# Batch 2 of a sliding-window attention plus mixer kernel: unpadded scores in two bursts, its u transposed by DMA

## The chip, the core and the metric

The kernel runs on one core of a Trainium2 chip. A core has five instruction streams that run beside each other and wait for each other by semaphores: TensorE (PE, matrix products out of SBUF into PSUM; a weight load goes ahead of each matmul), VectorE (DVE), ScalarE (ACT), GpSimd (POOL) and SyncE (SP, which here only issues DMAs). PSUM has eight banks of 2 KB in each partition. The metric is device time in microseconds (us), as the median of several runs; a run with the profiler on gives the trace, and has its own time.

## The reference

q, k and v are 8 batches x 8 heads x 576 positions x 64. Heads 0 to 3 see the last 32 positions; heads 4 to 7 see every fourth of the last 128. The attention output, 576 x 512 a batch, is the x of one mixer block: a token mix, then a channel mix.

```python
scores = scale * np.matmul(q, k.transpose(0, 1, 3, 2))
rel = pos[:, None] - pos[None, :]
mask_plain = (rel >= 0) & (rel < window)                       # window 32, heads 0-3
mask_dil = (rel >= 0) & (rel < window * dilation) & (rel % dilation == 0)   # dilation 4, heads 4-7
attn = softmax(where(mask, scores, -1e9)); x = attn @ v
h = np.maximum(xt @ w_tok1, 0.0) @ w_tok2                      # xt: x transposed, over 576 positions
u = x + h.transpose(0, 2, 1)
h2 = np.maximum(u @ w_ch1, 0.0) @ w_ch2                        # 512 -> 1536 -> 512
return u + h2
```

## The kernel before

All operands of matmuls are fp16, sums are fp32 in PSUM. A batch passes through these steps, each with its tile names:

- **Loads** (SP): q and k as `l_q`, `l_k` (two halves each), `lt` (last 64 positions of both), v as `l_vn`, `l_vt`, `l_vd`, `l_vx`. POOL casts them to fp16 (`c_q`, `c_k`, `c_t`, `vv`, `vt`).
- **Turning** q and k so that the 64 channels lie in the partitions, two heads (a pair `hp`) on top of each other. Batches 0 to 2 use PE transposes into PSUM (`tp_q`, `tp_k`), and DVE or ACT copy them out: keys to `kt`, queries to `qz`, which holds each head of the pair padded with zeros in the other head's 64 rows. From batch 3 on (`by_dma`) DMA transposes issued by SP write `qt`, `kr` and `tt`, and POOL places `kt` from them.
- **Scores**. Batches 0 to 2 (`scores_plain`, `scores_dil`) multiply over 128 rows, one head at a time, the padding hiding the other head; a piece is three yields for a pair: head 0, head 1, and a small bank `sm`. From batch 3 on `scores_twin` (line 465) multiplies over 64 rows: the two heads of a pair are two matmuls on the two halves of the array, one right behind the other. It does two pairs at a stretch (a burst) into six banks; two bursts make a batch. ACT exponentiates out of PSUM into `attp`, `attd`, `attt`, and POOL multiplies by the masks.
- **Values** (`values`): probabilities times v, with a row sum as the 65th column, into `av`; DVE takes the reciprocal (`rec`) and scales to `xn`. Heads 0 to 3 fill the first 256 columns of `xn`, heads 4 to 7 the others.
- **Token mix**: `h1p` (`emit_h1`, one call for 128 hidden units and 256 columns; so all eight heads are in before the last two calls), a relu to `h1`, then `up` (`emit_u`, blocks 4, 0, 1, 2, 3 of the positions), and u = `up` + `xn` as `u16` (blocks 0 to 3) and `u16t` (block 4, for two batches).
- **u transposed** (`uT`): batches 0 to 2 by PE (`emit_uT`, bank `tpu`), from batch 3 on (`turned`) by DMA transposes into `utm` and `utt`, of which ACT copies two quarters into `utd`.
- **Channel mix** (`gen_main`): twelve `gp` groups of four matmuls of 512 columns, each with a relu to `gt`; then `yp`, groups of twelve matmuls of 256 columns, DVE adds u into `o`, and SP stores it. An odd batch also does the block 4 of itself and of the batch before (`gt` tails, three groups of 16, and `yp` of block 4).

The order of the work is written out: for each batch b, `interleave` runs `gen_main(b)` (the channel mix, whose yields count modelled PE microseconds) and puts in between them the steps of later batches, each at a time t of that count: turning and scores of batch b+2, values, token mix and uT of batch b+1, casts and loads of batches b+2 and b+3. Each engine runs its own instructions in the order in which they were written, and SP is one such list too.

Banks: tag `fl` has three, `main` three, `sc` two, each handed round in turn. A tile in a bank waits until what was in it three tiles (`sc`: two) earlier has been read out. `h1p`, `up`, `av`, `tp` and `tpu` are in `fl`; `gp`, `gt` tails and `yp` are in `main`; a burst takes `sc`, `sc`, `fl`, `fl`, `fl`, `main`.

## Time and profile before

| | before |
|---|---|
| median of 3 runs | 290.61 us (290.55 to 290.86) |
| the profiled execution: its time, its span | 291.14 us, 289.2 us |
| mean granted TensorE clock | 0.997 |
| PE busy | 279.6 us, 97% of the span |
| ACT, DVE, POOL busy | 137.1, 130.0, 165.6 us |
| DMA | 52.11 MB, mean 180 GB/s |

In the timeline view each row is a group of like instructions: the start of the first (us from the span's start), the time from there to the end of the last, engine, line, operation, output and input tiles with sizes, the count, and in brackets the idle time before it and what ended it. Matmuls overlap: the next begins while the one before still drains. So the step from one row's start to the next row's start, and not the duration, says how long PE was held.

### The profile page before, as it was taken

How to read it: one execution, taken by the hardware profiler on the slowest of the kernel's cores; microseconds unless marked ns; L12 is line 12 of the kernel's file. 1: busy time of each engine (PE TensorE's matmuls, PEld its weight loads, DVE VectorE, ACT ScalarE, POOL GpSimd, SP SyncE). 2: the span in 40 equal slices, each digit the busy share in tenths (PEclk: the TensorE clock that was granted, in tenths of full speed). 3: DMA queues.
4: the chain of work that ended last, by engine and by line, in shares of the span. 5: the costliest groups of instructions: out<-in, count | busy, mean ns of one | idle time of the engine just before them, and what ended most of it. 6: DMA issues, size and time to landing. Idle time of an engine off the chain costs nothing.

```text
span 289.2 us, 7086 instructions
## 1 busy us (share of the span) xinstructions
PE 279.6 (97%) x2854; PEld 213.5 (74%) x2854; DVE 130.0 (45%) x275; ACT 137.1 (47%) x270; POOL 165.6 (57%) x227
## 2 busy tenths in 40 slices
PE   6999999999999999999999999999999999999994
PEld 2786576897676886688776976697776966896594
DVE  6775659356624138413741155415540274421022
ACT  2874572257553703574447614482446524225500
POOL 6980860576996599649962999279953920000000
PEclk9999999999999999999999999999999999999998
DMA  7999999973998987569897999399965220431023
GB/s 217 267 220 261 252 209 215 319 199 103 312 218 182 325 226 184 74 131 354 206 204 147 331 270 151 62 220 331 216 123 99 80 73 2 90 112 37 2 74 108
DMA packets 103472, 52.11 MB, mean 180 GB/s; under 512 B 71792, under 2 KB 102384, under 8 KB 103440
## 3 DMA queue, kind: packets, MB, share of 16 engines
q1 hardware_dynamic: 99200, 46.55, 64.8%
q0 software_dynamic: 2640, 3.94, 8.0%
q10 hardware_dynamic: 1600, 1.18, 1.4%
q8 instruction: 22, 0.36, 0.5%
q14 instruction: 10, 0.08, 0.1%
HBM read 37.07 MB, written 9.44 MB: 161 GB/s over the span
## 4 chain that ended last, share of the span: by engine, by line
PE 65%; DVE 1%; issue 0%
PE yp L735 25%; PE gp L716 22%; PE up L590 3%; PE gt L707 3%; PE yp L755 3%; PE h1p L578 3%; PE sc L475 2%; PE av L554 1%; PE h1p L576 1%; PE av L559 1%; PE up L601 1%; PE av L552 1%; PE yq L735 0%; PE av L564 0%; PE av L562 0%; DVE xn L112 0%
## 5 line engine op out<-in xcount | busy, mean ns | idle before, releaser
L735 PE MATMUL yp<-w,gt 128*128 128x256 f16 x756 | 87.4, 273 | 0.0
L106 ACT ACTIVATE gt<-gp 128x512 f16<-128x512 f32 x76 | 45.4, 597 | 79.9 <-PE gp L716 79.5
L735 PEld LDWEIGHTS <-gt 128*128 128x128 f16 x768 | 78.6, 106 | 6.3
L716 PEld LDWEIGHTS <-w 128*128 128x128 f16 x384 | 39.0, 114 | 19.6 <-issue 0.5
L112 POOL TENSOR_TENSOR attp<-attp,const 128x1280 f16<-128x1280 f16 x12 | 31.4, 2614 | 34.1 <-ACT attp L499 30.0
L745 DVE TENSOR_TENSOR o<-yp,u 128x512 f32<-128x512 f32 x31 | 21.5, 692 | 64.2 <-PE yp L735 57.0
L716 PE MATMUL gp<-utd,w 128*128 128x512 f16 x120 | 45.5, 380 | 0.0
L716 PE MATMUL gp<-utm,w 128*128 128x512 f16 x120 | 45.5, 379 | 0.0
L716 PE MATMUL gp<-uT,w 128*128 128x512 f16 x144 | 38.7, 379 | 0.0
L112 DVE TENSOR_TENSOR xn<-av,rec 128x320 f16<-128x320 f32 x64 | 31.5, 492 | 2.2
L112 POOL TENSOR_TENSOR attd<-attd,const 128x1024 f16<-128x1024 f16 x12 | 25.3, 2126 | 0.0
L596 DVE TENSOR_TENSOR u<-up,xn 128x512 f16<-128x512 f32 x26 | 17.9, 691 | 8.4 <-PE up L590 8.4
L102 POOL CAST c_q<-l_q 128x512 f16<-128x512 f32 x31 | 19.1, 619 | 2.8 <-DMA l_q<-in_q_dram 2.1
L102 POOL CAST c_k<-l_k 128x512 f16<-128x512 f32 x29 | 17.8, 616 | 1.9 <-DMA l_k<-in_k_dram 1.8
L567 DVE RECIPROCAL rec<-av 128x5 f32<-128x5 f32 x64 | 12.2, 191 | 14.9 <-PE av L564 14.7
L108 DVE TENSOR_SCALAR gt<-gp 128x512 f16<-128x512 f32 x20 | 13.7, 686 | 10.5 <-PE gp L716 10.1
L106 ACT ACTIVATE h<-h1p 128x256 f16<-128x256 f32 x29 | 11.1, 384 | 13.4 <-PE h1p L578 12.9
L392 PEld LDWEIGHTS <-kt 128*128 128x128 f16 x144 | 12.1, 103 | 3.9 <-DVE kt L314 1.4
L499 ACT ACTIVATE attp<-sc 128x480 f16<-128x480 f32 (+1 forms) x30 | 13.4, 526 | 3.0 <-PE sc L475 3.0
L366 POOL COPY kt<-kr 128x512 f16<-128x512 f16 x10 | 10.7, 1075 | 6.2 <-DMA kr<-c_k 6.1
L112 POOL TENSOR_TENSOR attt<-attt,const 128x512 f16<-128x512 f16 (+1 forms) x14 | 14.2, 1016 | 0.0
L605 DVE TENSOR_TENSOR u16t<-up,xn 64x512 f16<-64x512 f32 x7 | 4.8, 689 | 19.6 <-PE up L601 19.6
(135 smaller groups left out, 479.9 us busy)
## 6 DMA issues: line engine op xcount, KB each, us to landing
out_dram<-o SPq DMA_DIRECT2D x72, 128.0 KB, 2.7
l_q<-in_q_dram SPq DMA_DIRECT2D x15, 512.0 KB, 7.2
l_k<-in_k_dram SPq DMA_DIRECT2D x14, 512.0 KB, 7.5
l_vn<-in_v_dram SPq DMA_DIRECT2D x32, 128.0 KB, 6.3
l_vd<-in_v_dram SPq DMA_DIRECT2D x16, 256.0 KB, 4.5
w<-in_moe_w_ch_dram POOLq DMA_DIRECT2D x6, 512.0 KB, 7.6
lt<-in_q_dram SPq DMA_DIRECT2D x8, 128.0 KB, 4.3
l_vt<-in_v_dram SPq DMA_DIRECT2D x8, 128.0 KB, 4.7
```

The costliest lines, as they stand in the source:

```text
L102: eng.tensor_copy(out=out, in_=in_)
L106: nc.scalar.activation(out=out, in_=in_, func=AF.Relu)
L108: eng.tensor_scalar_max(out=out, in0=in_, scalar1=0.0)
L112: eng.tensor_tensor(out=out, in0=x, in1=y, op=ALU.mult)
L366: nc.gpsimd.tensor_copy(out=natural(kt[hp][:, 0:512]), in_=kra[:, hp].rearrange("p r m -> p m r"))
L392: nc.tensor.matmul(out=out, lhsT=lhsT, rhs=qz[hp][:, h, queries], start=hide is None, stop=True)
L499: nc.scalar.activation(out=out, in_=in_, func=AF.Exp, scale=0.125)
L567: nc.vector.reciprocal(out=rec[:, :, 0], in_=av[:, :, 64])
L596: nc.vector.tensor_tensor(out=u16(b, s), in0=blocks4(p), in1=blocks4(xn[b][:, s]), op=ALU.add)
L716: nc.tensor.matmul(out=p, lhsT=w3_block(cb, mb), rhs=uT[(b, cb)][0], start=(i == 0), stop=(i == 3))
L735: nc.tensor.matmul(out=p[:, c], lhsT=gta[:, mb, a0:m0 + 512:4] if half else gta[:, mb, a0:a0 + 128], rhs=w4[mb][:, c], start=(mb == 0), st ...
L745: nc.vector.tensor_tensor(out=blocks4(o32), in0=blocks4(p), in1=u16(b, s), op=ALU.add)
```

## The change

Batch 2 leaves the padded form. Its q and k are still turned by PE (`bare_steps`), but copied unpadded into `qt`, `kr`, `tt` and `kt`, and its scores are two bursts of `scores_twin`. The first burst (pairs 0 and 1) lies in `gen_main(0)`, between the blocks of batch 1's u and its transposes; the second (pairs 2 and 3) lies near the start of `gen_main(1)`. For batch 2 a burst takes `fl` for its first two banks and `sc` for the next two. `scores_twin` now yields after each exponential, and ACT begins with the bank of the tag `main` in every batch from 2 on. Batch 2's u goes by DMA transpose (`turned` is `b >= 2`); its steps, and with them everything else of stage 1, get new times. In stage 1 DVE takes nine of the twelve relus of `gp` (two before), and ACT takes four casts of batch 3's q from POOL. In batch 1 the quarter `cb == 3` of uT is copied by DVE and no longer by ACT.

```diff
+    def twinned(b):
+        return b >= 2
...
+    def bare_steps(b):
+
+        def tails():
+            p = bank("fl", 3, f"tp_t_{b}", FP16)
+            for hp in range(4):
+                nc.tensor.transpose(
+                    out=p[:, 128 * hp:128 * hp + 128],
+                    in_=c16[(b, "t")][:, 2 * hp:2 * hp + 2, :].rearrange("m h d -> m (h d)"), identity=ident)
+            t = p[:, 0:512].rearrange("p (x c) -> p x c", c=128)
+            nc.vector.tensor_copy(out=kta[:, :, 512:S], in_=t[:, :, 64:128])
+            nc.scalar.copy(out=tta, in_=t)
+
+        def turn_over(nm, hp):
+            p = bank("fl", 3, f"tp_{nm}_{b}_{hp}", FP16)
+            for r in range(4):
+                nc.tensor.transpose(
+                    out=p[:, 128 * r:128 * r + 128],
+                    in_=c16[(b, nm)][:, hp, r].rearrange("m h d -> m (h d)"), identity=ident)
+            grid = p[:, 0:512].rearrange("p (r m) -> p r m", r=4)
+            if nm == "q":
+                nc.scalar.copy(out=qta[:, hp], in_=grid)
+            elif hp < 2:
+                nc.vector.tensor_copy(out=natural(kt[hp][:, 0:512]), in_=grid.rearrange("p r m -> p m r"))
+            else:
+                nc.vector.tensor_copy(out=kra[:, hp], in_=grid)
+                nc.vector.tensor_copy(out=natural(kt[hp][:, 384:512]),
+                                      in_=grid[:, :, 96:128].rearrange("p r m -> p m r"))
...
     def scores_twin(b, g):
         tags = (("sc", 2), ("sc", 2), ("fl", 3), ("fl", 3), ("fl", 3), ("main", 3))
+        if b == 2:
+            tags = tags[2:4] + tags[0:2] + tags[4:6]
...
+        yield from small_exps(1)
+        if b == 2:
+            yield from small_exps(0)
+        for hp in (2 * g, 2 * g + 1):
+            for h in range(2):
+                main(hp, h)
+                if h and (g or b == 2):
+                    mask(hp)
+                    if b == 2 and hp % 2 == 0:
+                        mask_tails()
+                yield 0.0
+        if b > 2:
+            yield from small_exps(0)
...
     def emit_uT(b, cb):
-        eng = nc.scalar if cb == 2 or (b and cb == 3) else nc.vector
+        eng = nc.scalar if cb == 2 else nc.vector
...
     def turned(b):
-        return b >= 3
+        return b >= 2
...
     def gen_main(b):
-            relu(nc.vector if (mb % 2 == 1 if b == 0 else mb in (1, 5)) else nc.scalar, gta[:, mb, m0:m0 + 512], p)
+            relu(nc.vector if (mb % 2 == 1 if b == 0 else mb % 4 != 3 if b == 1 else mb in (1, 5)) else nc.scalar, gta[:, mb, m0:m0 + 512], p)
...
         if b == 0:
+            steps += mix_steps(1, 18.0, 20.6, 22.6, 31.4, 1.1)
+            steps += at(24.0, 0.3, cast_steps(2))
+            bare = bare_steps(2)
+            scores2 = score_steps(2, 29.6, 4.4, lag=0.25)
+            steps += [(t, 0.25, f) for t, f in zip((25.2, 25.9, 27.0, 27.6, 28.2, 34.8, 35.2, 35.6, 36.0), bare)]
+            steps += scores2[:10]
+            steps += at(34.0, 0.0, [lambda: emit_loads_qk(3)])
         elif b == 1:
+            va = value_steps(2, 0.0, 1.0)
+            steps += [(0.8 + 0.4 * i, c, f) for i, (_, c, f) in enumerate(scores2[10:])]
+            steps += [(t, c, f) for t, (_, c, f) in zip((2.2, 3.0, 4.8, 5.6, 8.2, 9.0, 10.4, 11.2), va)]
+            steps += mix_steps(2, 7.0, 12.4, 14.6, 24.4, 1.0, 5.6, 0.8)
+            steps += [(9.5 + 1.0 * i, 0.0, lambda i=i: cast_qk(3, "q", i, nc.scalar)) for i in range(4)]
+            steps += score_steps(3, 21.0, 4.6, lag=0.1)
+            steps += at(6.0, 0.0, [lambda: load_v(3)]) + at(20.8, 0.9, load_steps(4))
+            steps += at(11.0, 0.9, dma_steps(3)) + at(17.0, 0.4, place_steps(3))
```

Three places of the order follow. In tile names the first number after the name is the batch; `sc_2_0_5` is bank 5 of batch 2's burst 0, `up_1_2` is block 2 of batch 1's u, `tpu_1_2` its quarter 2 transposed. The last number is only the buffer's.

ACT, at the end of `gen_main(0)`, before:

```order
L594 CAST u16_1_1065<-up_1_2_1097 128x4x128
L100 COPY uT_1_2_1129<-tpu_1_2_1128 128x640
L100 COPY uT_1_3_1165<-tpu_1_3_1164 128x640
L100 COPY qz_64<-tp_q_2_0_1189 64x576 x2
L100 COPY kt_65<-tp_q_2_0_1189 128x64
L100 COPY qz_64<-tp_q_2_1_1221 64x576 x2
L100 COPY kt_65<-tp_q_2_1_1221 128x64
L428 ACTIVATE attp_73<-sc_2_0_0_1238 128x3x160
```

and with the change:

```order
L643 CAST u16_1_1065<-up_1_2_1113 128x4x128
L383 COPY qt_66<-tp_q_2_1_1139 128x512
L534 ACTIVATE attp_73<-sc_2_0_5_1172 128x2x128
L534 ACTIVATE attt_76<-sc_2_0_5_1172 128x2x2x64
L534 ACTIVATE attp_73<-sc_2_0_4_1171 128x2x128
L534 ACTIVATE attt_76<-sc_2_0_4_1171 128x2x2x64
L534 ACTIVATE attp_73<-sc_2_0_0_1167 128x3x160
L534 ACTIVATE attp_73<-sc_2_0_1_1168 128x3x160
L534 ACTIVATE attp_73<-sc_2_0_2_1169 128x3x160
L100 COPY uT_1_2_1224<-tpu_1_2_1223 128x640
L534 ACTIVATE attp_73<-sc_2_0_3_1170 128x3x160
```

Seven exponentials now stand ahead of the copy of batch 1's first transposed quarter. `tpu_1_2` takes the bank that `sc_2_0_0` had.

DVE, in `gen_main(1)`, up to the scaling of batch 2's last head, before:

```order
L112 TENSOR_TENSOR xn_2_1377<-av_2_4_1508,rec_2_4_1515 128x5x64
L108 TENSOR_SCALAR gt_93<-gp_1_5_1505 128x512
L567 RECIPROCAL rec_2_5_1532<-av_2_5_1525 128x5
L112 TENSOR_TENSOR xn_2_1377<-av_2_5_1525,rec_2_5_1532 128x5x64
L567 RECIPROCAL rec_2_6_1565<-av_2_6_1558 128x5
L112 TENSOR_TENSOR xn_2_1377<-av_2_6_1558,rec_2_6_1565 128x5x64
L567 RECIPROCAL rec_2_7_1594<-av_2_7_1587 128x5
L112 TENSOR_TENSOR xn_2_1377<-av_2_7_1587,rec_2_7_1594 128x5x64
```

and with the change:

```order
L112 TENSOR_TENSOR xn_2_1391<-av_2_4_1520,rec_2_4_1527 128x5x64
L108 TENSOR_SCALAR gt_93<-gp_1_5_1509 128x512
L616 RECIPROCAL rec_2_5_1540<-av_2_5_1533 128x5
L112 TENSOR_TENSOR xn_2_1391<-av_2_5_1533,rec_2_5_1540 128x5x64
L108 TENSOR_SCALAR gt_93<-gp_1_6_1546 128x512
L616 RECIPROCAL rec_2_6_1578<-av_2_6_1571 128x5
L112 TENSOR_TENSOR xn_2_1391<-av_2_6_1571,rec_2_6_1578 128x5x64
L616 RECIPROCAL rec_2_7_1591<-av_2_7_1584 128x5
L112 TENSOR_TENSOR xn_2_1391<-av_2_7_1584,rec_2_7_1591 128x5x64
```

The relu of `gp_1_6` now stands among the last heads, and those of `gp_1_0`, `gp_1_2` and `gp_1_4` stand ahead of this piece.

SP, from the loads of batch 3 to those of batch 4, with the change:

```order
L190 DMA l_k_3_1_1273<-in_k_dram 128x4x256
L803 DMA out_0_dram<-o32_0_3_1296 128x256 x2
L207 DMA l_vn_3_1482<-in_v_dram 128x4x64 x4
L207 DMA l_vt_3_1485<-in_v_dram 64x8x64
L207 DMA l_vd_3_1483<-in_v_dram 128x2x256 x2
L207 DMA l_vx_3_1484<-in_v_dram 128x4x64
L351 DMA_TRANSPOSE tt_68<-c_t_3_1480 128x4x128
L351 DMA_TRANSPOSE qt_66<-c_q_3_1544 128x8x128
L351 DMA_TRANSPOSE kr_67<-c_k_3_1507 128x8x128
L351 DMA_TRANSPOSE qt_66<-c_q_3_1544 128x8x128
L351 DMA_TRANSPOSE kr_67<-c_k_3_1507 128x8x128
L687 DMA_TRANSPOSE utm0_89<-u16_2_1648 128x16x128
```

Two things moved here. The store of batch 0's last block (`o32_0_3`) stood ahead of batch 3's q and k and now stands behind them; and the transpose of batch 2's u is new, ahead of batch 4's first load, which follows this piece.

More of the change, by code (lines that the diff above doesn't have):

```diff
@@ L358, in dma_steps @@
         return steps
+    def bare_steps(b):
[23 more added lines that the diff above has]
+                                      in_=grid[:, :, 96:128].rearrange("p r m -> p m r"))
+        return [tails] + [lambda nm=nm, hp=hp: turn_over(nm, hp) for hp in range(4) for nm in ("q", "k")]
     def place_steps(b):
@@ L648, in uT_place, with score_steps @@
             nc.scalar.copy(out=natural(uTd[:, cb - 2]), in_=uTm[i][:, cb].rearrange("p r m -> p m r"))
-    def score_steps(b, t0, dt, offs=(0.0, 0.7, 2.0), places=None):
+    def score_steps(b, t0, dt, offs=(0.0, 0.7, 2.0), places=None, lag=0.0):
         steps = []
-        if by_dma(b):
+        if twinned(b):
             for g in range(2):
-                for i, f in enumerate([scores_twin(b, g)] * 2):
-                    steps.append((t0 + g * dt, 0.86 * (i == 0), lambda f=f: next(f)))
+                f = scores_twin(b, g)
+                at = t0 + g * dt
+                steps.append((at, 0.86, lambda f=f: next(f)))
+                for i in range(7 if g else 9):
+                    steps.append((at + lag * (i + 1), 0.0, lambda f=f: next(f)))
             return steps
@@ L675, in value_steps, with mix_steps @@
         return steps
[L677 removed]
+    def mix_steps(b, t_h1, t_h1b, t_u, t_uT, du=1.0, turn=6.0, gap=2.6):
         h1 = [sb.tile([128, DM], FP16, tag="h1", bufs=4, name=f"h1_{b}_{jb}") for jb in range(2)]
```

80 lines of the change are left out of this document (34 added, 46 removed).

## The prediction

> **What bounds the kernel now.** First the page's part 1, then the busy time by stage: the stretch that the change rewrites (from batch 1's second block of u, at 54.65 us, to batch 2's first `gp`, at 106.39 us) and the rest after it.
>
> ```profile
> PE 279.6 (97%) x2854; PEld 213.5 (74%) x2854; DVE 130.0 (45%) x275; ACT 137.1 (47%) x270; POOL 165.6 (57%) x227
> 55.00:107.00 52.00, 51.19 (x563) 41.29 (x561) 23.25 (x48) 27.33 (x56) 40.53 (x50) 1.00 0.88 224
> 107.00:285.00 178.00, 177.82 (x1721) 134.99 (x1718) 70.07 (x145) 81.40 (x155) 94.68 (x114) 1.00 0.62 150
> ```
>
> PE is busy in 177.82 of the last 178.00 us, at a granted clock of 1.00, and no other engine reaches two thirds. So the end moves with PE alone: what is taken off PE's list before 106.39 us, or added to its waits, comes out at the end one for one, as long as the later stages find their inputs in time. Busy hides waits under about 0.2 us, since a matmul's duration overlaps the next; I take the steps between starts in PE's timeline instead.
>
> ```profile
> 54.65 0.38 PE L590 MATMUL up<-h,w 128*128 128x256 f16 x2
> ...
> 68.30 0.37 PE L392 MATMUL sc<-qz,kt 128*128 128x160 f16 x3
> 68.50 0.39 PE L309 MATMUL tp_k<-const,c_k 128*128 128x128 f16 x4
> ...
> 69.16 0.39 PE L392 MATMUL sm<-qz,kt 128*128 128x128 f16 x6
> 69.39 0.60 PE L716 MATMUL gp<-uT,w 128*128 128x512 f16 x2
> ...
> 70.96 0.39 PE L392 MATMUL sc<-qz,kt 128*128 128x128 f16 x4
> 71.19 0.39 PE L309 MATMUL tp_k<-const,c_k 128*128 128x128 f16 x4
> ...
> 71.68 0.28 PE L392 MATMUL sm<-qz,kt 128*128 128x64 f16 x4
> 71.80 0.60 PE L716 MATMUL gp<-uT,w 128*128 128x512 f16 x2
> ...
> 89.89 0.33 PE L624 MATMUL tpu<-const,u 128*128 128x128 f16 x3
> 90.41 0.23 PE L624 MATMUL tpu<-const,u 128*128 128x128 f16 x1 [0.19 <-DVE u L596]
> ...
> 91.34 0.39 PE L615 MATMUL tpu<-const,u 128*128 128x128 f16 x4
> 91.56 1.03 PE L755 MATMUL yp<-w,gt 128*128 128x512 f16 x4
> 92.42 0.39 PE L624 MATMUL tpu<-const,u 128*128 128x128 f16 x4
> ...
> 93.83 0.59 PE L475 MATMUL sc<-qt,kt 64*128 64x160 f16 x12
> 94.79 0.23 PE L475 MATMUL sc<-qt,kt 64*128 64x128 f16 x2 [0.37 <-DVE uT L102]
> ...
> 98.52 8.03 PE L735 MATMUL yp<-w,gt 128*128 128x256 f16 x72
> 106.39 0.59 PE L716 MATMUL gp<-uT,w 128*128 128x512 f16 x2
> ...
> 123.71 0.64 PE L475 MATMUL sc<-qt,kt 64*128 64x160 f16 x14
> ...
> 124.46 3.45 PE L735 MATMUL yp<-w,gt 128*128 128x256 f16 x30
> 127.84 0.62 PE L475 MATMUL sc<-qt,kr 64*128 64x128 f16 x16
> ...
> 128.51 1.72 PE L735 MATMUL yp<-w,gt 128*128 128x256 f16 x14
> ```
>
> PE's pace without waits is 0.109 us for 256 columns (72 from 98.52 to 106.39), 0.216 for 512 (4 from 91.56 to 92.42), 0.056 for 128 (4 from 91.34 to 91.56). The stretch lasts 106.39 - 54.65 = 51.74 us.
>
> **Work taken off PE.** *Scores.* A padded score piece holds PE 0.20 us (three of 160 columns), 0.23 (the small bank of a plain pair), 0.23 (four of 128) or 0.12 (its small bank). Batch 2 has 4, 2, 4 and 2 of them: 0.80 + 0.46 + 0.92 + 0.24 = 2.42 us. The bursts that replace them are the code of batch 4's, seen above: the second starts 0.10 us after the 30 `yp` matmuls ahead of it are through (124.46 + 30 x 0.109 = 127.74) and the next `yp` starts at 128.51, so it holds PE 0.77 us; the first 124.46 - 123.71 + 0.10 = 0.85. Together 1.62, a gain of **0.80 us**. The Trainium skill, in TensorEngine Tiling (Array Packing), Theoretical Speedup, gives two row tiles up to twice the speed; an estimate from that page would be 1.21 us, and a gain of 0.40 more. The rows contain the 0.1 us on either side of a burst, and I go by them.
>
> *Turning q and k.* 36 transposes before, 36 after: nothing. *u of batch 2.* Its 16 transposes (four groups of 0.22 us by the row at 91.34) leave PE: **0.90 us**. All else on PE's list in the stretch is the same by count. The work goes down by 1.70 us.
>
> **Waits that go.** The same counts give the old work of the stretch: 218 matmuls of 256 columns 23.8 us, 62 of 512 13.4, 120 of 128 (scores left out) 6.7, 60 of 65 at 0.03 1.8, scores 2.42, batch 3's bursts 1.62, in all 49.8. So PE waited 51.74 - 49.8 = **1.95 us** there. The two largest show above: 90.41, where three transposes should have held PE 0.17 us and took 0.52 (the last block of u was not added yet, 0.35), and 94.79 (twelve matmuls of a burst at some 0.034 should be through at 94.24; the banks of uT were still being copied, 0.55). All of these belong to code that is gone or has moved.
>
> **Waits that come.** I walk PE's new list from 54.65 with these rows of ACT, DVE, SP and POOL.
>
> ```profile
> 94.31 2.23 ACT L499 ACTIVATE attp<-sc 128x480 f16<-128x480 f32 x5 [0.87 <-PE sc L475]
> 96.39 0.43 ACT L499 ACTIVATE attt<-sc 128x256 f16<-128x256 f32 x1
> 96.65 0.44 ACT L499 ACTIVATE attp<-sc 128x256 f16<-128x256 f32 x1
> ...
> 98.34 2.06 ACT L499 ACTIVATE attd<-sc 128x512 f16<-128x512 f32 x4 [0.97 <-PE sc L475]
> ...
> 81.24 0.20 PE L564 MATMUL av<-vv,attt 128*128 128x65 f16 x1
> ...
> 81.48 0.20 DVE L567 RECIPROCAL rec<-av 128x5 f32<-128x5 f32 x1 [0.36 <-PE av L564]
> 81.71 0.49 DVE L112 TENSOR_TENSOR xn<-av,rec 128x320 f16<-128x320 f32 x1
> ...
> 70.14 0.68 DVE L108 TENSOR_SCALAR gt<-gp 128x512 f16<-128x512 f32 x1
> 70.74 0.91 DVE L102 COPY qz<-tp_q 64x576 f16<-64x576 f16 x2
> ...
> 68.54 0.61 SPq L196 DMA_DIRECT2D lt<-in_q_dram  x1
> ...
> 83.02 1.32 SPq L348 DMA_TRANSPOSE tt<-c_t  x1
> ...
> 63.21 0.41 POOL L102 CAST vt<-l_vx 128x256 f16<-128x256 f32 x1
> 67.67 2.61 POOL L112 TENSOR_TENSOR attp<-attp,const 128x1280 f16<-128x1280 f16 x1 [4.05 <-ACT attp L437]
> ...
> 89.19 1.07 POOL L366 COPY kt<-kr 128x512 f16<-128x512 f16 x1 [1.19 <-DMA kr<-c_k]
> ...
> 90.55 1.07 POOL L366 COPY kt<-kr 128x512 f16<-128x512 f16 x1
> ```
>
> A large exponential takes a step of 0.52 us in a row and 0.60 alone, a small one 0.27; a reader starts 0.24 us after the start of the last short matmul it waits for (81.24, 81.48); a relu on DVE takes a step of 0.60, a head (`rec` and `xn`) 0.63.
>
> (a) PE's new list up to the first burst is 4.6 us of work, so the burst would begin at 59.3. The six banks that it and the six groups just ahead of it need come back every 0.6 us or so; one, of `up_1_2` on ACT, is late by my walk: **0.2 us**. The burst runs 59.5 to 60.2.
>
> (b) Twelve `yp` matmuls later, at 61.6, `tpu_1_2` wants the bank of `sc_2_0_0`. ACT can start on the burst at 60.4, does four small exponentials (to 61.5) and then that one: free at 62.1, **0.5 us**. The queue behind it on PE is the whole of u's transposes; the next banks come back in time for them.
>
> (c) The second burst ends at 70.35, `gp_1_1` at 71.2, and `av_2_0` wants the bank of `sc_2_1_0`: ACT starts at 70.5, two small ones, then it: 71.65. **0.45 us**. The masks are not the limit: POOL's last cast of batch 2 ended at 63.62, where the burst's exponentials are nearly done, and a mask takes it 2.61 us; with the tails' mask behind it the first pair is ready some 4 us before it is needed.
>
> (d) The last two calls of `h1p` want all eight heads scaled. PE gets there at 81.5. DVE has `gp_1_5`'s relu from 78.7, then head 5, the relu of `gp_1_6`, heads 6 and 7: 0.60 + 0.63 + 0.60 + 0.63 + 0.69 with a short gap ahead of head 6 makes 81.95. **0.45 us**; behind it wait u of batch 2 and its transpose by DMA, which by my walk is copied out some 7 us before the first `gp` of batch 2.
>
> (e) Batch 3's first burst now stands before eight of the twelve matmuls of block 4's `yp`: PE reaches it at 90.5, where it was 93.83, and wants the second `kt` 0.2 us later. That copy ended at 91.62 (90.55 + 1.07). SP sends batch 3's q and k ahead of `o32_0_3` now, by my walk at 66.7 (68.54 before), but that store, about 1 us of issue, then stands ahead of v; so the transposes that began at 83.02 begin some 0.85 us earlier and `kt` is there at 90.8. **0.1 us**; bounds 0 and 0.9 (nothing gained on SP).
>
> With 0.4 us for small waits that such a walk does not see (as the two rows account for 0.90 of the old 1.95, small ones are common here), the new waits come to 0.2 + 0.5 + 0.45 + 0.45 + 0.1 + 0.4 = **2.1 us**; bounds 0 and twice that, since a wait of half a microsecond is worked out from steps that each err by 0.1 or 0.2.
>
> *At nothing:* seven more relus on DVE in stage 1 (its tasks from 69.6 to 82 sum to some 9 of 12.4 us, the relus 0.60 each; their cost where they come late is d); four casts of 0.6 us on ACT, in gaps of the relus that it gave up; the transpose of u ahead of batch 4's loads, which holds SP some 2 us: those loads are cast only after POOL's masks, which end after 104 us, and would have to come 6 us late to be seen.
>
> **Sum.** -1.70 of work, -1.95 of old waits, +2.1 of new ones: **-1.55 us**. The profiled execution took 291.14 us with a span of 289.2, and its 0.5 us over the median of 290.61 and what lies outside the span should not change: 290.61 - 1.55 = **289.05 us**.
>
> **The rivals.**
> 1. *The new waits do not come.* If the banks and DVE keep up, only small waits of 0.5 us remain: -1.70 - 1.95 + 0.5 = -3.15, 287.5 us. For it: after 107 us PE lost 0.2 us in 178. Against: (b) and (c) follow from the order of exponentials and their steps.
> 2. *Emptying PSUM becomes the bound.* All banks of a burst come back only when the whole burst has been read: 4 x 0.27 + 4 x 0.52 = 3.2 us for the first, 2.6 for the second, so `tpu_1_2` would wait 2.0 and `av_2_0` 1.9, that is 2.95 more: 292.0 us, slower. It decides from a wait of some 3.6 us in all. Against it: each tile's bank is handed on by itself. The Trainium skill, on the same page under PSUM Bottleneck, says that array tiles speed up TensorE but not the emptying of PSUM, which may become the limit, and wants ScalarE and VectorE both on it; here ACT alone reads the bursts.
> 3. *Batch 3's keys come late.* Four casts of its q now wait in ACT's list between relus, and SP holds `qt` and, behind it, `kr` until they are done. At 0.85 us early I have the first `kr` land at 88.3; each microsecond later is a microsecond of PE at the burst. It decides from 90.0 on (then the kernel is no faster); at 91.2, as if the second cast were done at 85 and not at 82, the time is 289.05 + 2.75 = 291.8 us, slower. Against: ACT has some 2 us of room there.
> 4. *DVE runs late in stage 1, or the pairs of batch 2 do not overlap as batch 4's do.* DVE's six relus ahead of the last head are 3.6 us, two of them were there before; if its gaps take up half of the 2.4 that are new, (d) is 1.2 and not 0.45; with 0.4 of the same kind at the adds of u, 290.2 us: no change to be seen.
>
> **How the numbers follow.** Forecast 0.55 (its own range, with new waits between 1.2 and 3.0 us, 288.1 to 290.0), rival 1 0.18, rival 2 0.05, rival 3 0.08, rival 4 0.14. A change of 0.2%, 0.58 us, is about what a measurement of this kernel can tell from none. Faster than 290.03: forecast and rival 1, 0.73; slower than 291.19: rivals 2 and 3, 0.13; the rest 0.14. The range takes rival 1's time and rival 4's with some room: 287.4 to 290.8.
>
> **What would show it.** In the changed profile PE's busy time falls by some 1.5 us and its bursts of batch 2 step through in 0.65 to 0.75 us. PE's rows show waits on ACT `attp` before the first `tpu` and on ACT `attd` before the first `av` of batch 2, on DVE `xn` before the third `h1p`, and the first burst of batch 3 begins near 90.5 with little wait on POOL. Batch 2's first `gp` comes near 104.8. I am wrong if those waits sum to under 1 or over 3.5 us, if that burst waits on POOL or DMA for more than 1 us, or if waits turn up after 107 us.

## The result, and the profile after

The changed kernel takes 288.74 us, the median of 4 runs (288.18 to 289.66), against 290.58 us for the kernel before (290.13 to 290.86): a ratio of 0.994, 95% interval 0.9915 to 0.9966. Measured again in the first round of experiments it took 288.2 us (6 runs, 287.65 to 289.31) against 290.35, ratio 0.9921 (0.9899 to 0.9942). It is faster by some 2 us; the forecast was 289.05, so 1.55.

Its profiled execution took 289.66 us with a span of 287.8. The busy time from the page's part 1, then the windows view of the rewritten stretch and of the rest:

```profile
PE 276.8 (96%) x2838; PEld 210.9 (73%) x2838; DVE 132.1 (46%) x278; ACT 134.0 (47%) x265; POOL 163.0 (57%) x221
```

```profile
55.00:105.00 50.00, 49.29 (x544) 38.94 (x542) 25.20 (x50) 24.64 (x52) 38.77 (x44) 1.00 0.92 228
106.00:284.00 178.00, 177.82 (x1715) 135.09 (x1713) 69.73 (x144) 81.41 (x155) 93.51 (x113) 1.00 0.65 154
```

The second row is the old one again: 177.82 busy of 178.00. From batch 2's first `gp` to the last matmul's start it is 178.90 us in both kernels, so nothing of what was won before that point was lost after it. What happened lies in the stretch, in PE's timeline of the changed kernel:

```profile
55.18 0.38 PE L639 MATMUL up<-h,w 128*128 128x256 f16 x2
...
58.10 0.38 PE L378 MATMUL tp_k<-const,c_k 128*128 128x128 f16 x4
58.59 0.38 PE L378 MATMUL tp_q<-const,c_q 128*128 128x128 f16 x4
...
59.69 0.82 PE L787 MATMUL yp<-w,gt 128*128 128x256 f16 x6
60.44 0.64 PE L510 MATMUL sc<-qt,kt 64*128 64x160 f16 x14
...
61.19 1.50 PE L787 MATMUL yp<-w,gt 128*128 128x256 f16 x12
62.65 0.38 PE L673 MATMUL tpu<-const,u 128*128 128x128 f16 x4
...
69.24 1.03 PE L768 MATMUL gp<-uT,w 128*128 128x512 f16 x4
70.20 0.62 PE L510 MATMUL sc<-qt,kr 64*128 64x128 f16 x16
...
70.86 1.06 PE L768 MATMUL gp<-uT,w 128*128 128x512 f16 x4
71.77 0.19 PE L603 MATMUL av<-vv,attp 128*128 128x65 f16 x1
...
80.93 1.03 PE L768 MATMUL gp<-uT,w 128*128 128x512 f16 x4
82.35 0.28 PE L625 MATMUL h1p<-xn,w1t 128*128 128x256 f16 x1 [0.39 <-DVE xn L112]
...
90.94 0.38 PE L510 MATMUL sc<-qt,kt 64*128 64x160 f16 x6
91.53 0.44 PE L510 MATMUL sc<-qt,kt 64*128 64x160 f16 x8 [0.21 <-POOL kt L399]
...
105.06 0.38 PE L768 MATMUL gp<-utd,w 128*128 128x512 f16 x1
```

Read by steps from start to start, as in the prediction: the stretch lasts 105.06 - 55.18 = 49.88 us, 1.86 less than the 51.74 of before (in the second profiled execution of the same kernel 49.58, so 2.16 less). Subtracting PE's pace without waits from every step splits it: waits of 1.77 us (2.01 before), and work that went down by 1.6 us, with the 0.10 us on either side of each burst counted as work.

PE's list ahead of the stretch is the same in all kernels here, and yet the stretch begins at 54.65 us before, at 55.18 and 53.55 in two executions of the changed kernel (1.63 of the 1.9 us between their spans), and between 53.45 and 55.65 in the other runs. Most of the spread of the times is there. So each experiment is read first by its stretch, which is free of it, and then by its time. A stretch comes from one profiled execution; the two of the changed kernel differ by 0.30 us, which is all in one wait, that for batch 3's `kt` (0.40 and 0.10).

**A correction to the description of the kernel.** It says that a tile gets the bank of the tile three (or two) before it, and, at the order of ACT, that `tpu_1_2` takes the bank of `sc_2_0_0`. The rule holds for the tags `main` and `sc`, whose turns the kernel's helper `bank` counts itself (`turn`). The tag `fl` is not counted there: all its tiles share one tag with three buffers, and for them the runs show that a new tile takes the bank that was *released first*, that is whose last reader stands first in the program. ACT's timeline of the changed kernel shows it:

```profile
61.38 0.38 ACT L534 ACTIVATE attp<-sc 128x256 f16<-128x256 f32 x1 [1.79 <-PE sc L510]
61.66 0.38 ACT L534 ACTIVATE attt<-sc 128x256 f16<-128x256 f32 x1
61.93 0.39 ACT L534 ACTIVATE attp<-sc 128x256 f16<-128x256 f32 x1
62.19 0.40 ACT L534 ACTIVATE attt<-sc 128x256 f16<-128x256 f32 x1
62.46 1.53 ACT L534 ACTIVATE attp<-sc 128x480 f16<-128x480 f32 x3
```

The exponential of `sc_2_0_0` is the first of the three at 62.46, and each takes 0.60 alone; `tpu_1_2` starts at 62.65, while it runs. What had ended just before, at 62.59, is the second small exponential of `sc_2_0_4`, the one small bank with the tag `fl`. Two of the prediction's waits rest on the wrong bank.

### The profile page after: what moved, and what is told of

It reads as the page before. It is cut to its first block, busy times and chain, and to the rows that moved or that the text cites. A ratio compares the mean times of both kernels' runs of the same rounds, so it can differ in the third digit from the quotient of the medians.

```text
span 287.8 us, 6995 instructions
## 1 busy us (share of the span) xinstructions
PE 276.8 (96%) x2838; PEld 210.9 (73%) x2838; DVE 132.1 (46%) x278; ACT 134.0 (47%) x265; POOL 163.0 (57%) x221
## 4 chain that ended last, share of the span: by engine, by line
PE 80%; DMA 8%; DVE 3%; POOL 3%; issue 2%; ACT 2%; ACTq 1%; SPq 0%; POOLq 0%; DVEq 0%
PE yp L787 29%; PE gp L768 24%; DMA l_vd<-in_v_dram 4%; PE h1p L627 4%; PE yp L807 3%; DMA l_k<-in_k_dram 3%; PE up L639 3%; PE sc L510 3%; PE gt L759 3%; DVE xn L112 1%; DMA kr<-c_k 1%; PE h1p L625 1%; PE av L608 1%; PE up L650 1%; PE av L603 1%
## 5 line engine op out<-in xcount | busy, mean ns | idle before, releaser
L106 ACT ACTIVATE gt<-gp 128x512 f16<-128x512 f32 x69 | 41.2, 597 | 76.3 <-PE gp L768 76.0
L768 PE MATMUL gp<-utd,w 128*128 128x512 f16 x144 | 54.7, 380 | 0.0
L768 PE MATMUL gp<-utm,w 128*128 128x512 f16 x144 | 54.6, 379 | 0.0
L768 PE MATMUL gp<-uT,w 128*128 128x512 f16 x96 | 25.8, 379 | 0.0
L108 DVE TENSOR_SCALAR gt<-gp 128x512 f16<-128x512 f32 x27 | 18.5, 686 | 13.6 <-PE gp L768 13.1
L534 ACT ACTIVATE attp<-sc 128x480 f16<-128x480 f32 (+1 forms) x36 | 16.1, 536 | 7.4 <-PE sc L510 7.4
L102 POOL CAST c_q<-l_q 128x512 f16<-128x512 f32 x27 | 16.8, 629 | 3.1 <-DMA l_q<-in_q_dram 3.1
L697 ACT COPY utd<-utm 128x512 f16<-128x512 f16 x12 | 12.8, 1135 | 4.1 <-DMA utm<-u 4.1
L102 POOL CAST vv<-l_vn 128x256 f16<-128x256 f32 x32 | 12.0, 420 | 4.3 <-DMA l_vn<-in_v_dram 4.1
L112 POOL TENSOR_TENSOR attt<-attt,const 128x512 f16<-128x512 f16 x12 | 14.0, 1165 | 0.0
```

The costliest lines, as they stand in the source:

```text
L102: eng.tensor_copy(out=out, in_=in_)
L106: nc.scalar.activation(out=out, in_=in_, func=AF.Relu)
L108: eng.tensor_scalar_max(out=out, in0=in_, scalar1=0.0)
L112: eng.tensor_tensor(out=out, in0=x, in1=y, op=ALU.mult)
L534: nc.scalar.activation(out=out, in_=in_, func=AF.Exp, scale=0.125)
L697: nc.scalar.copy(out=natural(uTd[:, cb - 2]), in_=uTm[i][:, cb].rearrange("p r m -> p m r"))
```

## The experiments

All kernels compute the whole of the reference. "Changed" is the changed kernel; diffs are against it where nothing else is said.

**Both bursts of batch 2 twice: is the end still PE's alone?**

```diff
-        for j in range(2):
+        for j in (0, 1) * (2 if b == 2 else 1):
```

(at both loops over `j` in `scores_twin`, so that each matmul of batch 2's bursts is issued a second time into the same bank)

> Both bursts of batch 2 compute their scores twice over, into the same banks. By the changed profile's rows the matmuls of the first hold PE 0.64 us and of the second 0.55, without the 0.1 us ahead and behind, which are not doubled. Main theory: PE work +1.19; the wait of 0.40 on batch 3's kt at its first burst goes, since PE comes there later: stretch 50.6 to 50.8, time +0.7 to +0.9 us. Rival (PE has slack beside the emptying of the banks, which sets the pace): stretch 49.9 to 50.2.

289.61 us against 290.35, ratio 0.9971 (0.9956 to 0.9987); stretch 51.40. PE's timeline:

```profile
59.82 1.06 PE L510 MATMUL sc<-qt,kt 64*128 64x160 f16 x26
...
61.21 1.50 PE L787 MATMUL yp<-w,gt 128*128 128x256 f16 x12
...
92.43 0.44 PE L510 MATMUL sc<-qt,kt 64*128 64x160 f16 x8 [0.52 <-POOL kt L399]
```

The first burst now holds PE from 59.82 to 61.21, 1.39 us and not 0.75; with the second the work rises by 1.21 us, and the stretch by 1.52 against 49.88 and 1.82 against 49.58. Work put on PE comes out at the end one for one; none of it is hidden. What the theory had wrong is the wait for batch 3's `kt`: PE came to it 1.2 us later and still waited, 0.71 us. POOL's timeline here, then SP's in the changed kernel and in the one with ACT's copy first (below):

```profile
89.97 1.07 POOL L399 COPY kt<-kr 128x512 f16<-128x512 f16 x1 [4.39 <-DMA kr<-c_k]
```

```profile
83.88 1.63 SPq L351 DMA_TRANSPOSE qt<-c_q  x1
```

```profile
83.96 1.25 SPq L351 DMA_TRANSPOSE qt<-c_q  x1
```

In this run the first `kr` came to POOL 5.06 us after its issue on SP at 84.91; in the others 3.4 to 3.6. In the changed kernel, where the wait was 0.40, the first `qt` held SP 1.63 us; in the run with ACT's copy first, where there is no wait, 1.25. But PE's coming counts as well. Here and in the run without the swap of banks (below) PE comes to this burst 36.97 us after the stretch's start; there the second `kt` is ready after 36.5 us and PE does not wait, here after 37.8. In the changed kernel it is ready after 36.3, and PE comes at 35.76. So the wait is what is left between two times: PE's coming, and the keys', which went from 35.3 to 37.8 us over the runs with this order on SP.

**Batch 2's u by PE, all else as changed.**

```diff
     def turned(b):
-        return b >= 2
+        return b >= 3
```

> The change with batch 2's u transposed by PE again. Main theory: 16 transposes of 0.056 us come back, 0.90 us, and their waits on the last add of u or on banks up to 0.3: stretch 50.8 to 51.1, time 0.9 to 1.3 us over the change. Rival (u's transposes lay beside waits, so moving them to DMA gave nothing): stretch 49.9, time as the change.

292.07 us against 290.35, ratio 1.0058 (1.0034 to 1.0081): slower than the kernel before. The stretch is 54.69 us, and neither theory had that. Of PE and of ACT, from the timelines, and then PE's columns by stage from the windows view (busy us of PE, of its weight loads, DVE, ACT and POOL with counts, then the granted clock):

```profile
94.93 0.29 PE L510 MATMUL sc<-tt,kt 64*128 64x64 f16 x8
97.25 0.38 PE L673 MATMUL tpu<-const,u 128*128 128x128 f16 x4 [2.02 <-ACT attd L534]
...
97.96 10.34 PE L787 MATMUL yp<-w,gt 128*128 128x256 f16 x78
```

```profile
95.62 2.06 ACT L534 ACTIVATE attd<-sc 128x512 f16<-128x512 f32 x4
```

```profile
95.20:97.20 2.00, 0.02 (x2) 0.05 (x1) 0.00 (x0) 1.86 (x5) 2.00 (x3) 1.00 0.75 200
98.90:102.00 3.10, 3.10 (x16) 2.24 (x15) 0.66 (x1) 0.00 (x0) 3.10 (x3) 0.50 1.16 315
102.50:104.00 1.50, 1.50 (x17) 1.38 (x15) 0.69 (x1) 0.00 (x0) 1.50 (x2) 1.00 0.89 203
```

In the changed order the last two groups of transposes fall right behind batch 3's second burst, whose banks of `fl` come back only when ACT has read the large ones: PE waits some 2.1 us, and 0.27 for the next. That is one surprise. The other follows: from 98.90 to 102.00 PE is busy throughout, but at a granted clock of 0.50, and at 1.00 again from 102.50. (The counts of the two rows take in matmuls that reach over their edges.) The 78 matmuls that start at 97.96 hold PE until 108.14, 10.18 us, where at 0.109 each they would take 8.50: 1.7 us are lost. So 0.90 of work, 2.4 of waits and 1.7 of slow clock make up the 4.8 to 5.1 us. The slow clock did not come every time. The mean granted clock of an execution is 0.992 to 0.994 in five of the ten and 1.00 in the other five, and the median times of the two fives are 293.08 and 291.51 us.

**Batch 2's u by PE at a place with free banks.**

```diff
     def turned(b):
-        return b >= 2
+        return b >= 3
...
-            steps += mix_steps(2, 7.0, 12.4, 14.6, 24.4, 1.0, 5.6, 0.8)
+            steps += mix_steps(2, 7.0, 12.4, 14.6, 20.4, 1.0, 5.6, 0.8)
...
-            steps += score_steps(3, 21.0, 4.6, lag=0.1)
+            steps += score_steps(3, 24.4, 4.6, lag=0.1)
```

> The changed kernel with u of batch 2 by PE again, but unlike in the run before of that kind at a place where the banks are free: its four groups of transposes among the matmuls of block 4's yp, and batch 3's two bursts behind them. So it is the change without its u part. Theory (u by PE is worth its 0.90 us, and the other 4 us of the run before were a wait for banks and the slow matmuls behind it): stretch 49.6-49.9 + 0.90 + 0.35 (last block of u, as in the kernel before) - 0.1 to 0.4 (batch 3's keys are no longer late) = 50.3 to 51.0 us, time 288.8 to 289.7, no idle time over 1 us and a granted clock of 1.00. Rival (u by PE is dear in this kernel wherever it stands, since its copies compete with ACT and DVE): a stretch of 51.5 or more.

288.95 us against 290.53, ratio 0.9944 (0.9923 to 0.9964); stretch 50.42, within the theory's bounds; no idle time over 0.6 us. PE's four groups of transposes, of which the first is shown, each take 0.22 us, without a wait:

```profile
89.50 0.39 PE L673 MATMUL tpu<-const,u 128*128 128x128 f16 x4
```

Against the stretch of 49.58 (where the wait for `kt` was 0.10; here it is gone) u by PE costs 0.84 to 0.94 us, which is its work. The other 4 us of the run before belonged to where it stood, not to what it was. This kernel is also the change without its u part: 51.74 - 50.42 = 1.32 us.

**The other part alone: the kernel before, with u of batch 2 by DMA** (diff against the kernel before)

```diff
     def turned(b):
-        return b >= 3
+        return b >= 2
...
-            steps += mix_steps(2, 10.8, 14.6, 17.2, 22.2)
+            steps += mix_steps(2, 10.8, 14.6, 17.2, 26.0)
```

> The kernel before with one part of the change alone: batch 2's u is transposed by DMA and its 16 transposes leave PE; its padded scores stay. Theory (work off PE comes out one for one, and the two largest old waits belonged to these transposes): -0.90 of work, -0.35 (last block of u not yet added) and up to -0.56 (banks of uT ahead of batch 3's burst) of the stretch's 51.74 us: 49.9 to 50.9 us, time 288.8 to 289.8. Rival (the old waits move to the next consumer and the transposes only filled them): stretch 51.2 to 51.8, no change.

289.26 us (12 runs) against 290.53, ratio 0.9961 (0.9947 to 0.9975); stretch 50.65, so 1.09 us won, in the theory's range. Both old waits, 0.35 and 0.56, are gone, and a new one of 0.70 stands at the end of the stretch. From PE's timeline and SP's:

```profile
104.76 0.38 PE L716 MATMUL gp<-utd,w 128*128 128x512 f16 x1 [0.54 <-ACT attt L499]
```

```profile
91.47 6.60 SPq L638 DMA_TRANSPOSE utm<-u  x1
```

Here the transpose is issued behind four of batch 4's loads; it holds SP for 6.60 us and lands 8.6 us after its issue (1.31 and 4.7 in the changed kernel). ACT's copies out of it then end at 102.1 us, its exponentials behind them at 104.7, and `gp` wants a bank that they read. The parts alone win 1.32 and 1.09; together they would be 2.41, and the changed kernel has 1.86 and 2.16. Its wait for batch 3's `kt`, 0.40 and 0.10, is a part that neither has alone; 0.15 us are left over. The sum is rough, since the wait of 0.70 at the end of this run is not in the changed kernel.

**The u transpose behind most of batch 4's loads on SP.**

```diff
-            steps += mix_steps(2, 7.0, 12.4, 14.6, 24.4, 1.0, 5.6, 0.8)
+            steps += mix_steps(2, 7.0, 12.4, 14.6, 31.2, 1.0, 15.6, 0.8)
```

> The DMA transpose of batch 2's u goes behind batch 4's loads on SP, not ahead of them, and its copies out of utm are put correspondingly later. Theory: the loads take the queue and the DMA engines for some 12 to 15 us (their bytes are moved at 180 GB/s or so), utm lands near 107 us, and batch 2's first gp, at 105 us before, waits for it: stretch 53 to 55.5 us, time 291.5 to 294. Rival (the transpose overlaps with the loads and has the 7 us of room that the prediction saw): no wait ahead of gp, stretch 49.5 to 50.2, time as the changed kernel's. The size of the wait also says how much of the change's gain hangs on that place in the queue.

297.04 us against 290.22, ratio 1.0248 (1.0224 to 1.0273), 8.8 us over the changed kernel's 288.2. The stretch is 56.31, above the theory's 53 to 55.5: it had the wait right in kind and too small. The transpose now stands behind eleven of batch 4's fourteen loads, and ACT's copies out of it stand later to match. From the timelines of SP, ACT and PE, then the windows view:

```profile
103.79 3.50 SPq L687 DMA_TRANSPOSE utm<-u  x1
```

```profile
108.79 2.05 ACT L697 COPY utd<-utm 128x512 f16<-128x512 f16 x2 [10.76 <-DMA utm<-u]
```

```profile
109.91 0.58 PE L768 MATMUL gp<-utd,w 128*128 128x512 f16 x1 [6.65 <-ACT utd L697]
```

```profile
109.91:112.00 2.09, 2.09 (x13) 1.06 (x13) 0.51 (x2) 0.93 (x1) 2.09 (x6) 0.50 0.90 286
115.00:116.00 1.00, 1.00 (x14) 0.66 (x13) 0.80 (x3) 0.14 (x1) 0.00 (x0) 1.00 1.03 204
```

Counted from the stretch's start it is issued 15.0 us later than in the changed kernel (50.19 us, 35.18), and `gp` waits 6.82 us. Then PE runs at a clock of 0.50 for nearly 5 us: from `gp`'s start to the last matmul's it is 181.23 us where every other kernel here has 178.9 to 179.0, so 2.3 us more. Wait and slow clock are 9.1 us. So the place in the queue decides: behind four of the loads, in the run above, u by DMA still won 1.09 us, behind eleven it loses 9.

**Batch 2's first two banks from `sc` and not from `fl`.**

```diff
-        if b == 2:
-            tags = tags[2:4] + tags[0:2] + tags[4:6]
```

> Batch 2's bursts take the banks in the order of the other batches (sc, sc, fl, fl, fl, main), so that the fl banks hold what ACT exponentiates third and fourth. Theory A, a new tile takes the bank that was released first: tpu_1_2 has sc_2_0_4's bank as now and waits 0.1; tpu_1_0 waits 0.5, av_2_1 0.8, less the 0.40 at batch 3's kt: stretch 50.7 to 50.9. Theory B, the prediction's turn-taking by order of allocation: tpu_1_2 waits until sc_2_0_2 is read, 1.6 us, and av_2_0 until sc_2_1_2 is, 1.5: stretch 52.3 to 52.6. Theory C, banks do not limit here: 49.9.

289.24 us against 290.35, ratio 0.996 (0.9943 to 0.9977); stretch 50.72. PE's timeline:

```profile
62.79 0.38 PE L662 MATMUL tpu<-const,u 128*128 128x128 f16 x4 [0.30 <-ACT attp L532]
...
72.45 0.19 PE L601 MATMUL av<-vv,attp 128*128 128x65 f16 x1 [0.60 <-ACT attd L532]
...
90.91 0.64 PE L508 MATMUL sc<-qt,kt 64*128 64x160 f16 x14
```

and of POOL, the second `kt` of batch 3:

```profile
89.33 1.07 POOL L399 COPY kt<-kr 128x512 f16<-128x512 f16 x1
```

The waits are 0.46 us at the *second* `fl` tile behind the first burst and 0.76 at the second behind the other. The first tile of each finds the small bank, released first; the second wants the bank of `sc_2_0_2`, whose exponential stands late. That is the rule of the correction above, in both bursts. It also speaks against the rival that banks come back only when a whole burst is read: then the first tile would wait most. Batch 3's burst at 90.91 comes 1.2 us later than in the changed kernel and finds its keys.

**ACT's copy of the turned tails ahead of DVE's.**

```diff
-            nc.vector.tensor_copy(out=kta[:, :, 512:S], in_=t[:, :, 64:128])
             nc.scalar.copy(out=tta, in_=t)
+            nc.vector.tensor_copy(out=kta[:, :, 512:S], in_=t[:, :, 64:128])
```

> Only the order of two copies out of the bank of batch 2's turned tails changes: ACT's copy to tt comes first, DVE's to kt second. Theory (two readers of one bank run one after the other, and PE's wait ahead of the first burst is that of ACT's later copies behind this one): PE's three waits between 56 and 59 us, 0.51 us in the changed kernel, fall to some 0.1; the stretch goes from 49.58-49.88 to 49.1-49.5 us, the time 0.3 to 0.5 us below the changed kernel's. Rival (ACT is simply full there, as point (a) of the prediction has it with the bank of up_1_2): the waits stay at 0.4 or more, stretch 49.6-49.9. Second rival (DVE's copy, now second, makes the next DVE reader late): the same sum turns up ahead of another tile of DVE.

288.3 us against 290.22, ratio 0.9936 (0.9915 to 0.9957); stretch 49.19. The timelines of DVE and ACT in the changed kernel, and ACT's in this one:

```profile
56.66 0.28 DVE L372 COPY kt<-tp_t 128x256 f16<-128x256 f16 x1
```

```profile
56.97 0.59 ACT L373 COPY tt<-tp_t 128x512 f16<-128x512 f16 x1 [1.66 <-DVE kt L372]
```

```profile
56.51 0.59 ACT L372 COPY tt<-tp_t 128x512 f16<-128x512 f16 x1 [0.73 <-PE tp_t L368]
```

In the changed kernel ACT starts at 56.97, when DVE's *read* of the same bank, itself queued behind an add, ended at 56.94: the two readers run one after the other. With ACT first it starts when PE is through, after 0.73 us of idle time and not 1.66, so 0.93 earlier. PE's waits ahead of the first burst fall from 0.51 to 0.25 us, not to 0.1: half the theory. What is left is 0.18 at `tp_q` and 0.07 at `up`. Of the 0.69 us between this stretch and 49.88 the other 0.40 is the wait for `kt`, which did not come in this execution; against 49.58 the gain is 0.39, 0.10 of it that wait. DVE's copy, now second, starts 1.48 us after the stretch's start, as in the changed kernel, so the second rival falls. The time, 288.3, is not below the changed kernel's 288.2 and 288.74: a gain of this size shows in the stretch only.

**The relus of stage 1 back on ACT.**

```diff
-            relu(nc.vector if (... else mb % 4 != 3 if b == 1 else mb in (1, 5)) else nc.scalar, ...)
+            relu(nc.vector if (... else mb in (1, 5)) else nc.scalar, ...)
```

> The relus of gp in stage 1 go back to their old engines: DVE two, ACT ten; all else as in the changed kernel. Theory (point (d): DVE's new relus make the heads' scaling late): the wait for xn ahead of the third h1p, 0.66 us with the small one before it, falls to 0.1 or less. ACT gets seven relus of some 0.6 us between 69 and 83 us, beside eight exponentials of the second burst, so that banks of main and fl come back later: new waits of 0.3 to 1.5 us on ACT (gt or attd) in that stretch. Sum: stretch 49.6 to 50.7 us. Rival 1 (xn is late because the averages themselves come late from PE): the wait stays at 0.4 or more and the stretch is 50.0 to 51.3. Rival 2 (ACT has room for all of it): stretch 49.0 to 49.3, time 0.5 us below the changed kernel's.

288.34 us against 290.22, ratio 0.9932 (0.9917 to 0.9947); stretch 49.87, as changed, with the same wait of 0.40 for `kt`. DVE and PE:

```profile
79.86 0.20 DVE L616 RECIPROCAL rec<-av 128x5 f32<-128x5 f32 x1 [0.61 <-PE av L613]
80.09 0.49 DVE L112 TENSOR_TENSOR xn<-av,rec 128x320 f16<-128x320 f32 x1
80.50 0.18 DVE L616 RECIPROCAL rec<-av 128x5 f32<-128x5 f32 x1
80.72 0.49 DVE L112 TENSOR_TENSOR xn<-av,rec 128x320 f16<-128x320 f32 x1
```

```profile
81.27 0.28 PE L625 MATMUL h1p<-xn,w1t 128*128 128x256 f16 x1 [0.39 <-DVE xn L112]
```

The theory falls. DVE is idle for 0.61 us before the last two heads, and PE waits for `xn` exactly as long as with the relus there (0.55 us in its steps). The cause is PE's own order: the sums of heads 6 and 7 stand right behind each other, DVE takes two heads one after the other, and `h1p` comes only four `gp` matmuls later. That was rival 1 in kind, though the stretch it gave (50.0 to 51.3) was too long, because ACT did have room for the relus, as rival 2 said.

**Three steps later.** ACT's copy first, as above, and two more edits:

```diff
-            steps += mix_steps(2, 7.0, 12.4, 14.6, 24.4, 1.0, 5.6, 0.8)
+            steps += mix_steps(2, 7.0, 12.8, 14.6, 24.4, 1.0, 5.6, 0.8)
...
-            steps += score_steps(3, 21.0, 4.6, lag=0.1)
+            steps += score_steps(3, 21.8, 4.6, lag=0.1)
```

> Three edits of the changed kernel together: ACT's copy of the tails first, the last two calls of h1p 0.4 us of modelled PE time later, and batch 3's first burst 0.8 us later, behind eight matmuls of block 4's yp. Theory (the three waits are each a late input with slack behind it, so that PE can do other work first): of 0.51 + 0.66 + 0.40 us some 0.3 are left; stretch 48.6 to 49.1 us, time 0.6 to 1.2 us below the changed kernel's, about 287.2 us. Rival (what is late there stays late: a later burst makes a later second burst and a later exponential, and later h1p a later u): each wait turns up one consumer further, stretch 49.4 to 50.0 us and the time the changed kernel's. If batch 3's kt follows PE, as the run with both bursts twice had it, the wait at that burst stays near 0.3.

287.26 us against 290.22, ratio 0.9896 (0.9879 to 0.9913); stretch 48.77. PE's timeline:

```profile
79.23 1.46 PE L768 MATMUL gp<-uT,w 128*128 128x512 f16 x6
80.65 0.28 PE L625 MATMUL h1p<-xn,w1t 128*128 128x256 f16 x1
```

With six `gp` matmuls between the last head and `h1p`, and not four, the wait falls from 0.55 to 0.12; the wait for `kt` is gone; no wait turns up further on. The theory holds, and its time was right to 0.1 us.

**Three more, one place each, and then one of them alone.** On top of the version just shown:

```diff
-            steps += [(t, 0.25, f) for t, f in zip((25.2, 25.9, 27.0, 27.6, 28.2, 34.8, 35.2, 35.6, 36.0), bare)]
+            steps += [(t, 0.25, f) for t, f in zip((25.2, 25.9, 27.0, 28.1, 28.7, 34.8, 35.2, 35.6, 36.0), bare)]
...
-            steps += mix_steps(1, 18.0, 20.6, 22.6, 31.4, 1.1)
+            steps += mix_steps(1, 18.0, 20.6, 22.6, 32.3, 1.1)
...
-            steps += mix_steps(2, 7.0, 12.8, 14.6, 24.4, 1.0, 5.6, 0.8)
+            steps += mix_steps(2, 7.4, 13.2, 14.6, 24.4, 1.0, 5.6, 0.8)
```

> The version with the three later steps, moved on by one place each: tp_q of pair 1 behind six more yp matmuls, the first transposes of batch 1's u behind six more, h1p two gp matmuls later. Theory (each remaining wait is a late input with slack behind it): of the 0.6 us of waits that are left there (0.18, 0.12, 0.11, 0.12 and 0.08) some 0.1 to 0.3 stay; stretch 48.3 to 48.6 us where that version had 48.77; time 0.2 to 0.5 us below it, 286.8 to 287.1 us. Rival (no slack: what is moved later makes its own consumer late, the first burst, gp_1_0 or up of batch 2): stretch 48.7 to 49.5.

288.0 us against 290.53, ratio 0.9903 (0.9882 to 0.9923); stretch 48.95, longer than 48.77: the rival. The four waits that were aimed at are gone, and PE's timeline has a new one of 0.42 us at `up` of batch 2, beside 0.24 and 0.10 at batch 2's next transposes of q and k:

```profile
82.76 0.38 PE L650 MATMUL up<-h,w 128*128 128x512 f16 x1 [0.26 <-ACT h L106]
```

With only the first of the three diffs:

> The version with the three later steps and one of the last run's moves alone: tp_q of pair 1 six yp matmuls later, right before tp_k of pair 1. Theory (that step alone has slack; the other two of the last run had none, and brought 0.24, 0.10 and 0.42 us back at tp_k, tp_q and up): the wait of 0.18 us goes and nothing comes, stretch 48.5 to 48.7 us, time 287.0 to 287.5. Rival (the first burst's keys and queries become late): 48.8 us or more, with a wait on DVE kt or ACT qt at the burst.

287.13 us against 290.25, ratio 0.9882 (0.9862 to 0.9902); stretch 48.59: the wait of 0.18 is gone and nothing came for it. This is the fastest kernel here, 1.1 to 1.6 us below the changed one by the medians. Its stretch and that of the version before differ by 0.18 us, too little for the times to tell.

## Why the prediction was right, and where it was not

The sign, the time (289.05 for 288.74 and 288.2) and the place were right: PE alone sets the end, and the 178.9 us behind the stretch did not change. By its steps:

- **Scores, 2.42 to 1.62 us.** Right. The bursts hold PE 61.19 - (59.69 + 6 x 0.109) = 0.85 and 70.86 - (69.24 + 4 x 0.216) = 0.76, together 1.61. The Trainium skill's factor of two (TensorEngine Tiling (Array Packing), Theoretical Speedup), 1.21 us by the prediction's estimate from it, would have been too good by 0.40: a burst starts 0.10 us late and what follows it 0.10 late, and these four gaps are just that difference.
- **u off PE, 0.90.** Right; the run with u by PE at a free place shows 0.84 to 0.94.
- **Old waits, 1.95.** Right in sum (2.01 by steps). That the two large ones belonged to u's transposes by PE is shown by the run with that part alone, where both are gone; the others, nearly 1 us, remained there, most of them at the padded scores and the values behind them.
- **New waits, 2.1.** Measured 1.77, close as a sum, but the pieces were not. *(a)* 0.2 was 0.51: the step "one, of `up_1_2` on ACT, is late" missed that two engines reading one bank take turns. Putting ACT first took half of it away. *(b)* 0.5 was 0.12 and *(c)* 0.45 was 0: both took the bank from the order of allocation; in `fl` it goes by the order of release, as the run without the swap shows. The sign "waits on ACT before the first `av`" was wrong with it. *(d)* 0.45 was 0.55, and the cause given, seven relus more on DVE, is refuted: without them the wait is as long. It is two heads in a row shortly before their consumer: with two `gp` matmuls more in between, 0.12 is left. *(e)* 0.1 was 0.40 and, in the second execution, 0.10; in other runs 0 to 0.71. Counted from the stretch's start SP began the transposes 1.09 us earlier than before (`tt` at 82.46 and 83.02), where 0.85 was forecast; 0.38 of it went in the first `qt`, 1.63 us and not 1.25. *Small ones*, 0.4: 0.19, of which 0.11 at the first `h1p`. That the sum came within 0.33 us is luck in part: 0.71 us too little in (a), (d) and (e) stands against 1.04 too much in the others.
- **Sum.** -1.55 was -1.86 and -2.16. Waits were forecast 0.15 us longer than before, and were 0.24 shorter: that is the mis-sized term.
- **The sign in PE's busy time.** It was to fall by some 1.5 us and fell by 2.8: by 1.8 in the stretch and by 1.0 ahead of it, where PE's list is the same. So that sign measures more than the change.
- **Hidden edits.** Seven relus at nothing: right, by the run that moved them back at the same stretch. Four casts on ACT at nothing: no run varied them, but ACT had room for seven relus beside them in that run. The u transpose at nothing, with 7 us of room, was right as well, and the cover is its place in the queue: behind eleven of the loads it costs 9 us.

Of the rivals, the first (no new waits, 287.5 us) is what the best version came near to: by moving the consumers of late inputs, the waits in the stretch go from 1.77 to 0.5 us. The second (PSUM emptied by whole bursts) is contradicted by the run without the swap. The third (batch 3's keys) is real but small, up to 0.7 us. The fourth is refuted in both halves: DVE with the cause of (d), and the pairs of batch 2 overlap as batch 4's do (0.85 and 0.76 us with the gap ahead, where 0.85 and 0.77 were taken from batch 4).

What stays open: why a DMA transpose of batch 3's q or k holds SP 1.25 us in one execution and up to 2.16 in another, and with it much of the wait for `kt`, 0 to 0.7 us. Nothing here varied the DMA traffic by itself. Nor did a run vary what makes the 0.10 us on either side of a burst.

## What to carry to other kernels

When work comes off the engine that is the bound, sum the work from steps in its timeline: it comes out to a tenth of a microsecond. Waits do not come out by walking an order on paper unless one knows which bank is handed on (here, where the kernel does not count the turns itself, the one released first) and that two readers of a bank may take turns; cost them as a sum with wide bounds, and look afterwards for consumers that stand two or three matmuls too near to a late input, since moving those was worth as much as half of the change. A transfer on a shared queue is free only at its place: ask what stands ahead of it.

## What the runs showed that was not expected

**A wait of PE can be paid for twice.** After some 2.1 us of waiting (u by PE behind a burst) the granted clock was 0.50 from about 98.7 to 102.2 us (0.74 from 98.50 to 99.00, 0.85 from 102.00 to 102.50), beginning some 1.5 us after PE had started again, and that cost 1.7 us; by their mean clock, only five of the ten executions had it. After 6.82 us (the late transpose) it was 0.50 at once, for nearly 5 us, and cost 2.3; all five executions have a mean clock of 0.983 to 0.988. Waits of up to 0.76 us left it at 1.00. The Trainium skill, in TensorE: Matmul & The Clock Gate, Part 1: The HAM clock gate, What's actually happening, has the clock go to half after an idle window of about 3.4 us and come back after as long a busy one. The fall in the second case agrees, though the clock came back only after 4.7 us. In the first it came back after some 3.4 us, which agrees, but PE had waited for less than that, and the clock fell all the same, late, and not every time.

**Two engines that read one PSUM bank took turns** (`kt` ends at 56.94, `tt` starts at 56.97, 0.93 us later than with the order turned round), though neither writes it. The Trainium skill, in PSUM — Partial Sum Buffer, PSUM bank collisions raise a hardware error, has it that two engines must not access one bank and quadrant at once, reads of ScalarE and VectorE included, and that software has to order them. The order seen here agrees; what happens without it was not tried.

**A DMA transpose's price was not the same at every place in the queue:** 1.31 us of SP and 4.7 to landing ahead of batch 4's loads (5.8 in the second execution of the same kernel), 3.50 and 5.0 behind eleven of them, 6.60 and 8.6 right behind four. These are one execution each, so how much of it is the place and how much the traffic of the moment is not shown.
